# Score products one period behind their operands, norms and softmax in more pieces, W' blocks stored from two tiles

## The chip, the core and the metric

The kernel runs on one core of a Trainium2 chip. The core's engines each work through a queue of their own, in order: TensorE for matmuls (PE in the profile, its weight loads PEld), VectorE (DVE), ScalarE (ACT), GpSimd (POOL) and SyncE (SP), which here issues every DMA. The metric is the device time of one launch in microseconds, lower is better.

## What is computed

Two steps of a network, in float32, for B = 4 batches of N = 6080 tokens and C = 256 channels: an attention between channels, and a feed-forward layer of width 2048 on its result.

```python
qn = q / (np.linalg.norm(q, axis=1, keepdims=True) + 1e-06)
kn = k / (np.linalg.norm(k, axis=1, keepdims=True) + 1e-06)
s = kn.transpose(0, 2, 1) @ qn / tau
s = s - s.max(-1, keepdims=True)
a = np.exp(s)
a /= a.sum(-1, keepdims=True) + 1e-09
x = (v @ a).reshape(B * N, C)
h = x @ w_in
out = np.maximum(0.01 * h, h) @ w_out
```

The scores s of a batch are 256 x 256 and sum over all 6080 tokens, so a batch's attention matrix a is known only when all its q and k have been read.

## The kernel before

**Folding.** v @ a @ w_in is computed as v @ W', with W' = a @ w_in made once per batch. So the main loop multiplies v, laid out channel by token, with W' (256 x 2048), applies the leaky step, and multiplies with w_out.

**Precision.** Each float32 operand is split into a high part (a cast to float32r) and a low part (the rest), and a product takes three matmul passes: high by high, high by low, low by high. Splits cost ACT or DVE a cast and DVE a subtraction.

**Tiles and periods.** Tokens come in 24 tiles, six per batch: five of 2 x 512 and one of 2 x 480. For each tile the hidden width is walked in eight pairs p. One pass of the body of the inner loop is called a period here; a batch has 48 of them. A period computes four hidden blocks (C11, C22, C21, C12) by seven products of blocks (`block_product`, L517, three matmuls each) instead of eight: A11, S2, S3 and A22 add up in the bank ps_x, A12 goes to ps_y, S1 and S4 to ps_z. ACT copies ps_x away in between (`taken`, L544), DVE adds ps_y or ps_z (`add`, L538), and `leaky` does the activation and the split on ACT (L528, L529) and DVE (L531). The 24 matmuls with w_out (`ffn_out`, L563) run one period later; a period's PE queue has them in portions of 5, 5, 8 and 6 between the blocks (`out(n)`). At the end of a tile, finished outputs are copied to o_sb (L575) and stored.

**What is fitted in.** While a batch's 48 periods run, the next batch's scores are made: 48 chunks of 128 tokens. For each chunk ACT casts q and k (`cast`, L154) and squares them (L146), DVE subtracts (`low`, L158) and sums the squares (L149), and PE multiplies (`product`, L176) into the bank ps_s. Then come the norms by Newton steps (`norms`), the scaling of the scores and softmax (`scaled`, `exps`, `normed`), four transposes (`turn`, L279), and W' in four blocks j: two products per block (L383), two sums of sub-blocks, and for each of two pairs p = 2j and 2j + 1 the parts `begin` (blocks A11, A12 and A22, declared 1.0) and `rest` (S1 to S4, declared 1.2). Each pair's seven blocks, high and low, are stored to w_dram, and `w_load` brings them back as the tile w_split when the main loop needs them. Batch 0 uses its first W' blocks straight from w_split.

**What sets the order.** These steps wait in queues `todo` for ACT, DVE and PE, each with a declared length. `slot(queue, room)` takes steps off the head of a queue as long as the head's length fits into the room that is left; a head that doesn't fit holds back what is behind it. A step may put further steps, also at the head. In one period the slots lie like this (adds and leaky steps in their places):

```python
add(y); slot("dve", 1.3); out(5); slot("pe", 1); leaky(C11); slot("dve", 2.2)
S2; taken; slot("act", 1.8); S1; out(5); slot("pe", 1); S3; taken; add(z); slot("dve", 1.3)
out(8); slot("pe_late", 1); leaky(C22); A22; S4; add(z); leaky(C21); slot("dve", 0.8); leaky(C12)
```

`at(w, ...)` lists what is put into the queues at the start of period w. The opening, ahead of the first period, has batch 0's scores and the first block of W'; the conversion of w_in and w_out from 64 to 32 bits runs in it and in the first periods. Instructions outside these chains (loads, stores, the copies to o_sb) are placed by the framework's scheduler. An instruction waits until the buffer that it overwrites is free: w_new has two buffers, the high and the low half of one pair.

Of the kernel before, what the change touches and what calls it, by code (L numbers as in the profile page):

```python
# [31 lines left out]
def channel_attention_ffn(  # L32
# [17 lines left out]
    nc = tc.nc  # L50
# [49 lines left out]
    def f32(ap):  # L100
        return ap.bitcast(F32)


    class Scores:
# [10 lines left out]
        def begin(self, acc, s):  # L115
            self.acc, self.s = acc, s
# [83 lines left out]
                    )  # L200
            return mm

        def norms(self):
            n = 2 * CH
            x = small.tile([P, n], F32, name="nx")
            nc.vector.tensor_copy(out=x, in_=self.n_ps[:, 0:n])
# [4 lines left out]
            y = small.tile([P, n], F32, name="ny")  # L211
            nc.vector.tensor_scalar(
                out=y.bitcast(I32), in0=half, scalar1=-1.0, scalar2=RSQRT_MAGIC, op0=ALU.mult, op1=ALU.add
            )
            t = small.tile([P, n], F32, name="nt")
            for _ in range(3):
                nc.vector.tensor_tensor(out=t, in0=x, in1=y, op=ALU.mult)
                nc.vector.scalar_tensor_tensor(out=t, in0=t, scalar=-0.5, in1=y, op0=ALU.mult, op1=ALU.mult)
                nc.vector.scalar_tensor_tensor(out=y, in0=t, scalar=1.5, in1=y, op0=ALU.add, op1=ALU.mult)
            nc.vector.tensor_tensor(out=t, in0=x, in1=y, op=ALU.mult)  # L220
            nc.vector.tensor_scalar(out=t, in0=t, scalar1=1e-6, scalar2=None, op0=ALU.add)
            rn = small.tile([P, n], F32, name="rn")
            nc.vector.reciprocal(out=rn, in_=t)
            self.rk = small.tile([P, CH], F32, name="rk")
            nc.vector.tensor_scalar(
                out=self.rk, in0=rn[:, CH:n], scalar1=rtau[:, 0:1], scalar2=None, op0=ALU.mult
            )
            self.diag = small.tile([P, CH, P], F32, name="diag")
            for h in range(CH):
                last = nc.vector.tensor_scalar(  # L230
                    out=self.diag[:, h, :], in0=ident, scalar1=rn[:, h:h + 1], scalar2=None, op0=ALU.mult
                )
            return last

        def rows_mm(self):
# [4 lines left out]
                )  # L240
            return mm

        def scaled(self):
            self.rq = small.tile([P, C], F32, name="rq")
            nc.vector.tensor_copy(out=self.rq, in_=self.r_ps[:, 0:C])
            s = small.tile([P, CH, C], F32, name="s_sb")
            for h in range(CH):
                nc.vector.scalar_tensor_tensor(
                    out=s[:, h, :], in0=self.s[:, h * C:(h + 1) * C], scalar=self.rk[:, h:h + 1], in1=self.rq,
                    op0=ALU.mult, op1=ALU.mult,  # L250
                )
            self.nm = small.tile([P, CH], F32, name="nm")
            self.e = s
            return nc.vector.tensor_reduce(out=self.nm, in_=s, axis=AX.X, op=ALU.max, negate=True)
# [68 lines left out]
    class Conversions:  # L323
# [9 lines left out]
        def split(self):  # L333
            raw, split = self.loaded.pop(0)
            split(raw)
# [63 lines left out]
    def w_parts(b, j):  # L399

        HT = TW // 2
        a = [a_sb[b, j, h] for h in range(CH)]
        a21, a11, a22, a12 = a[0][:, 0:HT], a[0][:, HT:TW], a[1][:, 0:HT], a[1][:, HT:TW]
        s12, s34 = w_tmp("w_s"), w_tmp("w_s")
        s1, s2, s3, s4 = s12[:, 0:HT], s12[:, HT:TW], s34[:, 0:HT], s34[:, HT:TW]

        def sums(*of):
            for out, x, y, op in of:
                last = nc.vector.tensor_tensor(out=out, in0=x, in1=y, op=op)
            return last  # L410
# [5 lines left out]
        def split(k, w, *blocks):  # L416
            ks = slice(k * P, (k + 1) * P)
            for src, x0, n in blocks:
                src = src[:, ks] if n == 1 else src.rearrange(two, s=2)[:, :, ks]
                hi, lo = (x.rearrange(two, s=NS)[:, x0:x0 + n, :] for x in w)  # L420
                hi, lo = (x[:, 0, :] if n == 1 else x for x in (hi, lo))
                nc.vector.tensor_copy(out=hi, in_=src)  # L422
                last = nc.vector.tensor_tensor(out=lo, in0=src, in1=f32(hi), op=ALU.subtract)
            return last

        for k in range(2):
            p, w = 2 * j + k, []

            def begin(k=k, w=w, p=p):
                if b == 0:  # L430
                    w_split[0, p] = w_tile()
                    w += [w_split[0, p][:, x].rearrange("p s f -> p (s f)") for x in range(2)]
                else:
                    w += [work.tile([P, NS * P], F32R, name="w_new", bufs=2) for _ in range(2)]
                return split(k, w, (a11, A11, 1), (a[1], A22, 2))
# [141 lines left out]

    todo = {"act": deque(), "dve": deque(), "pe": deque(), "pe_late": deque()}  # L580
    steps = {}

    def at(w, fn, *args):
        steps.setdefault(w, []).append((fn, args))
# [10 lines left out]
    def put(queue, length, fn, then=(), first=False):  # L595


        def run():
            ins = fn()
            for entry in then:  # L600
                if entry[0] == "call":
                    entry[1](*entry[2:])
                else:
                    put(*entry)
            return ins

        (todo[queue].appendleft if first else todo[queue].append)((length, run))
# [102 lines left out]
    for b in range(1, B):  # L710
        w0 = (b - 1) * WPB
        sc = scores[b]
        done = FILL * G if b == 1 else 0
        begin_at, span = (NPAIR, 26) if b == 1 else (2, 32)
        when = {j: w0 + begin_at + (j - done) * span // (NCHUNK - done) for j in range(done, NCHUNK)}
        for i in range(done // G, len(sc.groups)):
            at(max(w0, when[i * G] - 3), lambda sc=sc, i=i: sc.load(i, qk_raw()))
        for j in range(done, NCHUNK):
            at(when[j], chunk_work, sc, j)
        e = w0 + begin_at + span + 1  # L720
        at(e, norm_work, sc)
        at(e + 1, row_work, sc)
        at(e + 2, turn_work, sc)
        at(e + 1, win_load, 0)
        at(e + 3, w_work, b, 0)


    sc, nxt = scores[0], scores[1]
# [30 lines left out]
            conv.split()  # L759
    sc.sums()  # L760
    sc.norms_mm()
    after["dve"] = sc.norms()
    with tc.issue_after(after["load"].ins):
        for i in range(min(2, FILL)):
            nxt.load(i, qk_raw())
    sc.rows_mm()
    after["scaled"] = sc.scaled()
    sc.exps()
    after["normed"] = sc.normed()
# [114 lines left out]
```

## Time and profile before

| | |
|---|---|
| three runs | 2280.37, 2281.03, 2281.41 us, median 2281.03 |
| the profiled execution | 2281.35 us |
| its span, first to last instruction | 2279.6 us |
| mean granted clock of TensorE | 0.987 |
| DMA | 324.74 MB, 142 GB/s over the span |
| idle time of PE in the first 200 us, longest group | 15.9 us in 4 waits for DVE's w_split |

The profile gives, for one execution, each engine's busy time, the chain of work that ended last, groups of instructions by line with their mean duration and the idle time of the engine just ahead of them, and who waited for whom. A wait is put down to the semaphore that came last. A row of the timeline has start, length, engine, line, operation, tiles (written, then read), shape, count, and in brackets the idle time ahead and what ended it.

### The profile page before, as it was taken

To read this page: it belongs to the slowest core of one execution; us is meant where nothing else is said; L and a number is where in the kernel's file an instruction comes from. 1 tells how busy PE (TensorE), PEld (TensorE's weight loads), DVE (VectorE), ACT (ScalarE), POOL (GpSimd) and SP (SyncE) were. 2 spreads that over 40 slices of the span, in tenths; PEclk is the share of its full clock that TensorE was granted. 3 is DMA by queue.
4 is the path that set the end of the run, shared out by engine and by line. 5 is a ranking of instruction groups with operands and counts; after the bars stand their busy time and mean duration, and the time that the engine had idled before them with its cause. 6 is when DMAs were issued, how large, how long until landed. Compare 5 with 4: busy or idle time off the path is not lost.

```text
span 2279.6 us, 27326 instructions
## 1 busy us (share of the span) xinstructions
PE 2204.1 (97%) x9940; PEld 1820.4 (80%) x9940; DVE 1494.0 (66%) x2651; ACT 1491.0 (65%) x2563; POOL 2.8 (0%) x10
## 2 busy tenths in 40 slices
PE   9689999999999999999999999999999999999999
PEld 7467888887878888888787888888788788888887
DVE  7986667666666666666666666676657555655554
ACT  6556767765557777776556777777655566666665
POOL 0000000000000000000000000000000000000000
PEclk9799999999999999999999999999999999999999
DMA  9435344342653434434364344343354432332331
GB/s 355 142 140 194 118 144 143 131 146 85 231 184 109 155 127 136 155 114 139 136 215 150 119 145 163 109 155 126 118 180 153 149 118 97 118 134 81 133 106 44
DMA packets 93975, 324.74 MB, mean 142 GB/s; under 512 B 10385, under 2 KB 16017, under 8 KB 93841
## 3 DMA queue, kind: packets, MB, share of 16 engines
q1 hardware_dynamic: 93840, 323.00, 40.8%
q8 instruction: 78, 1.28, 0.2%
q14 instruction: 57, 0.46, 0.1%
HBM read 264.50 MB, written 58.46 MB: 142 GB/s over the span
## 4 chain that ended last, share of the span: by engine, by line
PE 82%; DVE 10%; ACT 5%; DMA 1%; issue 1%; SPq 0%; DVEq 0%
PE ps_o L563 38%; PE ps_x L517 20%; PE ps_z L517 10%; PE ps_y L517 5%; PE ps_s L176 4%; DVE h L538 3%; DVE g_split L531 3%; ACT h L528 2%; ACT g_split L529 2%; PE ps_o L171 2%; PE ps_s L383 1%; DMA w_dram<-w_new 1%; ACT h L544 1%; DVE qk_split L158 1%; DMA f_raw<-in_w_out_dram 0%
## 5 line engine op out<-in xcount | busy, mean ns | idle before, releaser
L563 PE MATMUL ps_o<-g_split,w_out_split 128*128 128x512 f32 (+1 forms) x4608 | 1178.8, 392 | 0.0
L563 PEld LDWEIGHTS ps_o<-g_split,w_out_split 128*128 128x128 f32 x4608 | 870.7, 189 | 181.0
L531 DVE TENSOR_TENSOR g_split<-h,g_split 128x512 fp32r<-128x512 f32 (+1 forms) x768 | 525.6, 684 | 373.0 <-ACT g_split L529 371.2
L517 PE MATMUL ps_x<-v_split,w_split 128*128 128x512 f32 (+1 forms) x2304 | 660.8, 395 | 32.4 <-DVE w_split L422 15.9
L544 ACT COPY h<-ps_x 128x512 f32<-128x512 f32 (+1 forms) x576 | 334.7, 581 | 366.7 <-PE ps_x L517 365.8
L528 ACT ACTIVATE h<-h 128x512 f32<-128x512 f32 (+1 forms) x576 | 362.1, 629 | 321.8 <-DVE h L538 321.4
L517 PEld LDWEIGHTS ps_x<-v_split,w_split 128*128 128x128 f32 x2304 | 425.0, 190 | 124.0 <-ACT h L544 16.9
L529 ACT CAST g_split<-h 128x512 fp32r<-128x512 f32 (+1 forms) x768 | 473.5, 617 | 24.1
L538 DVE TENSOR_TENSOR h<-ps_z,h 128x512 f32<-128x512 f32 (+1 forms) x384 | 262.1, 683 | 342.1 <-ACT h L544 336.4
L517 PE MATMUL ps_z<-v_split,w_split 128*128 128x512 f32 (+1 forms) x1152 | 326.2, 392 | 15.6 <-DVE h L538 15.6
L517 PEld LDWEIGHTS ps_z<-v_split,w_split 128*128 128x128 f32 x1152 | 217.3, 189 | 65.0 <-DVE h L538 18.1
L517 PE MATMUL ps_y<-v_split,w_split 128*128 128x512 f32 (+1 forms) x576 | 164.4, 394 | 0.6 <-ACT w_a L393 0.6
L538 DVE TENSOR_TENSOR h<-ps_y,h 128x512 f32<-128x512 f32 (+1 forms) x192 | 131.5, 685 | 4.9 <-PE ps_y L517 3.0
L176 PEld LDWEIGHTS ps_s<-qk_split 128*128 128x128 f32 x804 | 113.9, 188 | 25.5 <-DVE qk_split L158 14.7
L176 PE MATMUL ps_s<-qk_split 128*128 128x256 f32 x804 | 123.2, 285 | 8.1 <-DVE qk_split L158 8.1
L517 PEld LDWEIGHTS ps_y<-v_split,w_split 128*128 128x128 f32 x576 | 110.4, 192 | 24.1 <-ACT w_a L393 1.1
L528 ACT ACTIVATE h<-ps_x 128x512 f32<-128x512 f32 (+1 forms) x192 | 113.2, 590 | 8.8 <-PE ps_x L517 8.6
L482 DVE TENSOR_TENSOR v_split<-v_raw,v_split 128x512 fp32r<-128x512 f32 (+1 forms) x144 | 98.7, 687 | 4.7
L149 DVE TENSOR_TENSOR sq_acc<-sq_acc,sq 128x512 f32<-128x512 f32 x141 | 96.4, 684 | 0.0
L158 DVE TENSOR_TENSOR qk_split<-qk_raw,qk_split 128x512 fp32r<-128x512 f32 x134 | 91.8, 685 | 0.0
L146 ACT ACTIVATE sq<-qk_raw 128x512 f32<-128x512 f32 x141 | 88.5, 632 | 1.4 <-DMA qk_raw<-in_k_dram 1.4
L154 ACT CAST qk_split<-qk_raw 128x512 fp32r<-128x512 f32 x134 | 82.9, 619 | 0.0
(101 smaller groups left out, 729.2 us busy)
## 6 DMA issues: line engine op xcount, KB each, us to landing
w_split<-w_dram SPq DMA_DIRECT2D x184, 896.0 KB, 4.6
qk_raw<-in_q_dram SPq DMA_DIRECT2D x92, 256.0 KB, 3.5
qk_raw<-in_k_dram SPq DMA_DIRECT2D x92, 256.0 KB, 3.9
w_dram<-w_new SPq DMA_DIRECT2D x48, 448.0 KB, 2.9
v_raw<-in_vT_dram SPq DMA_DIRECT2D x40, 512.0 KB, 5.7
out_dram<-o_sb SPq DMA_DIRECT2D x80, 256.0 KB, 3.4
win<-win_dram SPq DMA_DIRECT2D x24, 512.0 KB, 3.7
w_dram<-w_split SPq DMA_DIRECT2D x16, 448.0 KB, 3.5
```

The lines of the kernel that those rows point to most:

```text
L146: return nc.scalar.activation(out=out, in_=self.chunk(j), func=AF.Square)
L149: return nc.vector.tensor_tensor(out=self.acc[0], in0=self.acc[0], in1=sq, op=ALU.add)
L158: return nc.vector.tensor_tensor(out=sp[:, :, 1, :], in0=self.chunk(j), in1=f32(sp[:, :, 0, :]), op=ALU.subtract)
L176: mm = nc.tensor.matmul(out=s, lhsT=sp[:, 1, y, hs], rhs=sp[:, 0, z, :], start=False, stop=last and n == 2, skip_group_check=True,)
L482: last = nc.vector.tensor_tensor(out=sp[:, 1, 0:w], in0=src, in1=f32(sp[:, 0, 0:w]), op=ALU.subtract)
L517: mm = nc.tensor.matmul(out=ps[:, 0:n], lhsT=w[:, x, a, :], rhs=sp[:, y, 0:n], start=first and k == 0, stop=k == 2, skip_group_check=True,)
L528: nc.scalar.activation(out=out[:, 0:n], in_=h[:, 0:n], func=AF.Prelu, alpha=0.01)
L529: issued["act"] = nc.scalar.copy(out=sp[:, 0, 0:n], in_=out[:, 0:n])
L531: issued["dve"] = nc.vector.tensor_tensor(out=sp[:, 1, 0:n], in0=out[:, 0:n], in1=f32(sp[:, 0, 0:n]), op=ALU.subtract)
L538: issued["dve"] = nc.vector.tensor_tensor(out=h[:, 0:n], in0=ps[:, 0:n], in1=h[:, 0:n], op=ALU.add)
L544: issued["act"] = nc.scalar.copy(out=h[:, 0:n], in_=ps[:, 0:n])
L563: issued["pe"] = nc.tensor.matmul(out=o_ps[i][j][h][:, 0:n], lhsT=wo[:, x, f, h * P:(h + 1) * P], rhs=sp[:, y, 0:n], start=p == 0 and earl ...
```

## The change

Score products go to a queue of their own, `pe_next`, which is emptied into PE's queue at the start of the next period. The norms become three steps (the copy out of PSUM, two Newton steps, the rest) and the softmax's scaling two, with declared lengths of 1.8 and 2.0 for the long ones and 1.1 for the division. The scores of a batch are spread over one period less, while norms, rows, transposes and W' are put at e, e + 2, e + 4 and e + 5, against e, e + 1, e + 2 and e + 3 before, with e one period earlier. For batches 1 to 3 a pair's seven W' blocks go to two tiles of one buffer each, w_first (three blocks, high and low) and w_rest (four), each stored by one DMA as soon as it is full; batch 0 stores a pair by one DMA for two. No arithmetic is changed.

```diff
-        def norms(self):
-            n = 2 * CH
-            x = small.tile([P, n], F32, name="nx")
-            nc.vector.tensor_copy(out=x, in_=self.n_ps[:, 0:n])
+        def norms_taken(self):
+            self.nx = small.tile([P, 2 * CH], F32, name="nx")
+            return nc.vector.tensor_copy(out=self.nx, in_=self.n_ps[:, 0:2 * CH])
+
+        def newton(self, x, y, t, n):
+            for _ in range(n):
...
+        def norms_begun(self):
+            x, n = self.nx, 2 * CH
             half = small.tile([P, n], I32, name="nhalf")
...
-            for _ in range(3):
...
+            return self.newton(x, self.ny, self.nt, 2)
+
+        def norms(self):
+            x, y, t, n = self.nx, self.ny, self.nt, 2 * CH
+            self.newton(x, y, t, 1)
...
+        def rows_taken(self):
+            self.rq = small.tile([P, C], F32, name="rq")
+            return nc.vector.tensor_copy(out=self.rq, in_=self.r_ps[:, 0:C])
+
         def scaled(self):
-            self.rq = small.tile([P, C], F32, name="rq")
-            nc.vector.tensor_copy(out=self.rq, in_=self.r_ps[:, 0:C])
...
-            def begin(k=k, w=w, p=p):
+            def blocks(x0, n, name, k=k, w=w, p=p):
+
+                if b == 0:
+                    return [w_split[0, p][:, x, x0:x0 + n, :] for x in range(2)]
+                w.append(work.tile([P, 2, n, P], F32R, name=name, bufs=1))
+                return [w[-1][:, x] for x in range(2)]
+
+            def store(x0, n, w=w, p=p):
+                if b:
+                    nc.sync.dma_start(
+                        out=w_dram[b, p][:, :, x0 * P:(x0 + n) * P],
+                        in_=f32(w[-1].rearrange("p x s f -> p x (s f)")),
+                    )
+
+            def begin(k=k, p=p, blocks=blocks, store=store):
                 if b == 0:
                     w_split[0, p] = w_tile()
-                    w += [w_split[0, p][:, x].rearrange("p s f -> p (s f)") for x in range(2)]
-                else:
-                    w += [work.tile([P, NS * P], F32R, name="w_new", bufs=2) for _ in range(2)]
-                return split(k, w, (a11, A11, 1), (a[1], A22, 2))
-
-            def rest(k=k, w=w, p=p):
-                last = split(k, w, (s12, S1, 2), (s34, S3, 2))
-                for x in range(2):
-                    nc.sync.dma_start(out=w_dram[b, p][:, x], in_=f32(w[x]))
+                x0 = min(A11, A22)
+                last = split(k, blocks(x0, 3, "w_first"), x0, (a11, A11, 1), (a[1], A22, 2))
+                store(x0, 3)
+                return last
+
+            def rest(k=k, p=p, blocks=blocks, store=store):
+                last = split(k, blocks(S1, 4, "w_rest"), S1, (s12, S1, 2), (s34, S3, 2))
+                store(S1, 4)
+                if b == 0:
+                    w = w_split[0, p]
+                    nc.sync.dma_start(
+                        out=w_dram[0, p].rearrange("p x f -> p (x f)"), in_=f32(w.rearrange("p x s f -> p (x s f)"))
+                    )
                 return last
...
-            ("dve", 0.75, lambda: sc.low(j), [("pe", 1, lambda: sc.product(j))]),
+            ("dve", 0.75, lambda: sc.low(j), [("pe_next", 1, lambda: sc.product(j))]),
...
-        put("pe_late", 1, sc.norms_mm, [("dve", 0.5, sc.norms, (), True)])
+        put("pe_late", 1, sc.norms_mm, [
+            ("dve", 0.5, sc.norms_taken, [("dve", 1.8, sc.norms_begun, [("dve", 2.0, sc.norms)], True)], True),
+        ])
...
-            ("dve", 0.5, sc.scaled, [("act", 0.6, sc.exps, [("dve", 0.6, sc.normed, (), True)], True)], True),
+            ("dve", 0.5, sc.rows_taken, [
+                ("dve", 1.8, sc.scaled, [("act", 0.6, sc.exps, [("dve", 1.1, sc.normed, (), True)], True)], True),
+            ], True),
...
-        begin_at, span = (NPAIR, 26) if b == 1 else (2, 32)
+        begin_at, span = (NPAIR, 25) if b == 1 else (2, 31)
...
-        at(e + 1, row_work, sc)
-        at(e + 2, turn_work, sc)
+        at(e + 2, row_work, sc)
+        at(e + 4, turn_work, sc)
         at(e + 1, win_load, 0)
-        at(e + 3, w_work, b, 0)
+        at(e + 5, w_work, b, 0)
...
         for p in range(NPAIR):
+            todo["pe"].extend(todo["pe_next"])
+            todo["pe_next"].clear()
```

The next rows are DVE's queue at three places, before and in the change (L531 becomes L560, L538 becomes L567, L575 becomes L604). In these rows h is a hidden block, g_split its split after the leaky step.

First, from the leaky steps that close period 36 of batch 0's 48 on into the next, the softmax of batch 1. Before:

```order
L245 COPY rq<-ps_y 128x256
L248 SCALAR_TENSOR_TENSOR s_sb<-ps_s,rk,rq 128x256 x2
L254 TENSOR_REDUCE nm<-s_sb 128x2
L531 TENSOR_TENSOR g_split<-h,g_split 128x512
L538 TENSOR_TENSOR h<-ps_y,h 128x512
L267 TENSOR_SCALAR den<-den 128x2
L268 RECIPROCAL den<-den 128x2
L270 TENSOR_SCALAR s_sb<-s_sb,den 128x256 x2
```

In the change:

```order
L255 COPY rq<-ps_y 128x256
L560 TENSOR_TENSOR g_split<-h,g_split 128x512
L567 TENSOR_TENSOR h<-ps_y,h 128x512
L560 TENSOR_TENSOR g_split<-h,g_split 128x512
L260 SCALAR_TENSOR_TENSOR s_sb<-ps_s,rk,rq 128x256 x2
L266 TENSOR_REDUCE nm<-s_sb 128x2
L567 TENSOR_TENSOR h<-ps_z,h 128x512
L279 TENSOR_SCALAR den<-den 128x2
L280 RECIPROCAL den<-den 128x2
L282 TENSOR_SCALAR s_sb<-s_sb,den 128x256 x2
```

The scaling moved from ahead of a period's last leaky step to behind the next period's first one, and the division behind that period's first addition from ps_z.

Second, in period 40, the first of the batch's last tile (480 wide), from the leaky step of C11 on; w_a and w_s are blocks and sums of W'. Before:

```order
L531 TENSOR_TENSOR g_split<-h,g_split 128x480
L422 CAST w_new<-w_s 128x256 x2
L423 TENSOR_TENSOR w_new<-w_s,w_new 128x256 x2
L575 COPY o_sb<-ps_o 128x512
L422 CAST w_new<-w_a 128x128
L422 CAST w_new<-w_a 128x256
L423 TENSOR_TENSOR w_new<-w_a,w_new 128x128
L423 TENSOR_TENSOR w_new<-w_a,w_new 128x256
L538 TENSOR_TENSOR h<-ps_z,h 128x480
```

In the change:

```order
L560 TENSOR_TENSOR g_split<-h,g_split 128x480
L433 CAST w_first<-w_a 128x128
L433 CAST w_first<-w_a 128x256
L434 TENSOR_TENSOR w_first<-w_a,w_first 128x128
L434 TENSOR_TENSOR w_first<-w_a,w_first 128x256
L433 CAST w_rest<-w_s 128x256 x2
L434 TENSOR_TENSOR w_rest<-w_s,w_rest 128x256 x2
L567 TENSOR_TENSOR h<-ps_z,h 128x480
L604 COPY o_sb<-ps_o 128x512
```

A pair's two parts now follow each other behind the leaky step, and the addition from ps_z stands ahead of the copy to o_sb; the next pair's first part comes behind that copy.

Third, in the next batch's first period, where the last pair of W' (p = 7) is made behind the rest of pair 6. Before:

```order
L422 CAST w_new<-w_s 128x256 x2
L423 TENSOR_TENSOR w_new<-w_s,w_new 128x256 x2
L531 TENSOR_TENSOR g_split<-h,g_split 128x512
L422 CAST w_new<-w_a 128x128
L422 CAST w_new<-w_a 128x256
L575 COPY o_sb<-ps_o 128x480
L423 TENSOR_TENSOR w_new<-w_a,w_new 128x128
L423 TENSOR_TENSOR w_new<-w_a,w_new 128x256
L422 CAST w_new<-w_s 128x256 x2
L423 TENSOR_TENSOR w_new<-w_s,w_new 128x256 x2
L538 TENSOR_TENSOR h<-ps_z,h 128x512
```

In the change:

```order
L433 CAST w_rest<-w_s 128x256 x2
L434 TENSOR_TENSOR w_rest<-w_s,w_rest 128x256 x2
L560 TENSOR_TENSOR g_split<-h,g_split 128x512
L433 CAST w_first<-w_a 128x128
L433 CAST w_first<-w_a 128x256
L434 TENSOR_TENSOR w_first<-w_a,w_first 128x128
L434 TENSOR_TENSOR w_first<-w_a,w_first 128x256
L433 CAST w_rest<-w_s 128x256 x2
L434 TENSOR_TENSOR w_rest<-w_s,w_rest 128x256 x2
L567 TENSOR_TENSOR h<-ps_z,h 128x512
L604 COPY o_sb<-ps_o 128x480
```

The instructions stand as before, but in two tiles, and the copy to o_sb now comes behind the addition.

More of the change, by code (lines that the diff above doesn't have):

```diff
@@ L201, in norms_mm @@
             return mm
-        def norms(self):
-            n = 2 * CH
-            x = small.tile([P, n], F32, name="nx")
-            nc.vector.tensor_copy(out=x, in_=self.n_ps[:, 0:n])
+        def norms_taken(self):
[3 more added lines that the diff above has]
+            for _ in range(n):
+                nc.vector.tensor_tensor(out=t, in0=x, in1=y, op=ALU.mult)
+                nc.vector.scalar_tensor_tensor(out=t, in0=t, scalar=-0.5, in1=y, op0=ALU.mult, op1=ALU.mult)
+                last = nc.vector.scalar_tensor_tensor(out=y, in0=t, scalar=1.5, in1=y, op0=ALU.add, op1=ALU.mult)
+            return last
+        def norms_begun(self):
+            x, n = self.nx, 2 * CH
             half = small.tile([P, n], I32, name="nhalf")
@@ L210, in norms @@
             )
-            y = small.tile([P, n], F32, name="ny")
+            self.ny = small.tile([P, n], F32, name="ny")
             nc.vector.tensor_scalar(
-                out=y.bitcast(I32), in0=half, scalar1=-1.0, scalar2=RSQRT_MAGIC, op0=ALU.mult, op1=ALU.add
+                out=self.ny.bitcast(I32), in0=half, scalar1=-1.0, scalar2=RSQRT_MAGIC, op0=ALU.mult, op1=ALU.add
             )
-            t = small.tile([P, n], F32, name="nt")
-            for _ in range(3):
-                nc.vector.tensor_tensor(out=t, in0=x, in1=y, op=ALU.mult)
-                nc.vector.scalar_tensor_tensor(out=t, in0=t, scalar=-0.5, in1=y, op0=ALU.mult, op1=ALU.mult)
-                nc.vector.scalar_tensor_tensor(out=y, in0=t, scalar=1.5, in1=y, op0=ALU.add, op1=ALU.mult)
+            self.nt = small.tile([P, n], F32, name="nt")
+            return self.newton(x, self.ny, self.nt, 2)
+        def norms(self):
+            x, y, t, n = self.nx, self.ny, self.nt, 2 * CH
+            self.newton(x, y, t, 1)
             nc.vector.tensor_tensor(out=t, in0=x, in1=y, op=ALU.mult)
@@ L414, in w_parts, with split @@
         two = "p (s f) -> p s f"
-        def split(k, w, *blocks):
+        def split(k, to, at, *blocks):
             ks = slice(k * P, (k + 1) * P)
@@ L419, in split @@
                 src = src[:, ks] if n == 1 else src.rearrange(two, s=2)[:, :, ks]
-                hi, lo = (x.rearrange(two, s=NS)[:, x0:x0 + n, :] for x in w)
-                hi, lo = (x[:, 0, :] if n == 1 else x for x in (hi, lo))
+                hi, lo = (x[:, x0 - at, :] if n == 1 else x[:, x0 - at:x0 - at + n, :] for x in to)
                 nc.vector.tensor_copy(out=hi, in_=src)
@@ L427, in w_parts @@
             p, w = 2 * j + k, []
-            def begin(k=k, w=w, p=p):
+            def blocks(x0, n, name, k=k, w=w, p=p):
[10 more added lines that the diff above has]
+            def begin(k=k, p=p, blocks=blocks, store=store):
                 if b == 0:
                     w_split[0, p] = w_tile()
-                    w += [w_split[0, p][:, x].rearrange("p s f -> p (s f)") for x in range(2)]
-                else:
-                    w += [work.tile([P, NS * P], F32R, name="w_new", bufs=2) for _ in range(2)]
-                return split(k, w, (a11, A11, 1), (a[1], A22, 2))
-            def rest(k=k, w=w, p=p):
-                last = split(k, w, (s12, S1, 2), (s34, S3, 2))
-                for x in range(2):
-                    nc.sync.dma_start(out=w_dram[b, p][:, x], in_=f32(w[x]))
+                x0 = min(A11, A22)
+                last = split(k, blocks(x0, 3, "w_first"), x0, (a11, A11, 1), (a[1], A22, 2))
+                store(x0, 3)
+                return last
+            def rest(k=k, p=p, blocks=blocks, store=store):
[6 more added lines that the diff above has]
+                    )
                 return last
@@ L576, in ffn_out @@
                     nc.sync.dma_start(out=outT[h * P:(h + 1) * P, n0:n0 + n], in_=o[:, 0:n])
-    todo = {"act": deque(), "dve": deque(), "pe": deque(), "pe_late": deque()}
+    todo = {"act": deque(), "dve": deque(), "pe": deque(), "pe_late": deque(), "pe_next": deque()}
     steps = {}
@@ L761, in channel_attention_ffn @@
     sc.norms_mm()
+    sc.norms_taken()
+    sc.norms_begun()
     after["dve"] = sc.norms()
@@ L766, in channel_attention_ffn @@
     sc.rows_mm()
+    sc.rows_taken()
     after["scaled"] = sc.scaled()
```

## The prediction

> **What bounds the kernel now.** The page comes first: the span, the busy times and the chain that ended last.
>
> ```profile
> span 2279.6 us, 27326 instructions
> PE 2204.1 (97%) x9940; PEld 1820.4 (80%) x9940; DVE 1494.0 (66%) x2651; ACT 1491.0 (65%) x2563; POOL 2.8 (0%) x10
> PE 82%; DVE 10%; ACT 5%; DMA 1%; issue 1%; SPq 0%; DVEq 0%
> ```
>
> PE is busy for 97% and holds 82% of the chain; the other engines come into it only where PE stands. The change takes away no matmul, so all that it can win is PE's idle time and what follows from it. The waits of PE, cut at 200 us, say where that is (columns: total us, times, longest). This is all of PE's idle time behind 200 us:
>
> ```profile
> PE ps_z L517 <- DVE h L538: 15.6, 6, 3.8
> PE ps_s L176 <- DVE qk_split L158: 8.1, 18, 0.8
> PE ps_x L517 <- ACT h L544: 4.5, 3, 1.5
> PE ps_s L279 <- DVE s_sb L270: 4.1, 3, 1.4
> ```
>
> They sum to 32.3 us, and each group is one per batch or a few per tile. The waits ahead of 200 us belong to the opening, in which batch 0's scores, the weight conversion and the first W' run; there the order on PE, DVE and ACT is the same before and after, so I put that stretch at 0.
>
> To the idle time comes the clock. The table by windows gives, in its columns, the length, the busy time of PE, PEld, DVE, ACT and POOL with counts, the granted clock and the DMA share. The first three are the stretches behind the three longest waits; the fourth is the 3.41 us (half of what a drop lasts) ahead of the second of them, and the last holds most of the 2.47 us wait that ends at 580.25:
>
> ```profile
> 670.64:677.47 6.83, 5.87 (x14) 4.77 (x15) 4.07 (x7) 4.47 (x8) 0.00 (x0) 0.50 0.80 288
> 1227.01:1233.84 6.83, 6.16 (x15) 4.96 (x16) 3.77 (x7) 4.66 (x8) 0.00 (x0) 0.50 0.81 295
> 1783.39:1790.21 6.82, 6.04 (x15) 4.85 (x16) 3.88 (x7) 4.65 (x8) 0.00 (x0) 0.50 0.81 291
> 1223.60:1227.01 3.41, 1.19 (x6) 0.65 (x4) 2.68 (x10) 0.43 (x1) 0.00 (x0) 1.00 0.67 249
> 578.48:581.90 3.42, 1.66 (x7) 1.42 (x8) 2.68 (x8) 1.65 (x3) 0.00 (x0) 1.00 0.40 152
> ```
>
> Half clock for 5.87 + 6.16 + 6.04 = 18.07 us of matmuls costs half of that, 9.0 us. The stretch with 1.19 us of PE work lost the clock, the one with 1.66 us kept it. The ceiling is thus 32.3 + 9.0 = 41.3 us, 1.8% of the time.
>
> **Score products (8.1 us).** The low half of a chunk's split (L158) is computed just ahead of the product that reads it:
>
> ```profile
> 229.72 0.69 DVE L158 TENSOR_TENSOR qk_split<-qk_raw,qk_split 128x512 fp32r<-128x512 f32 x1
> 230.46 0.86 PE L176 MATMUL ps_s<-qk_split 128*128 128x256 f32 x5 [0.78 <-DVE qk_split L158]
> 510.57 0.84 PE L517 MATMUL ps_y<-v_split,w_split 128*128 128x512 f32 x3
> 511.25 1.31 PE L563 MATMUL ps_o<-g_split,w_out_split 128*128 128x512 f32 x5
> ```
>
> With the change a product enters PE's queue at the next period's start, and its first place there lies behind that period's ps_x and ps_y blocks and five output matmuls: the last two rows alone are 0.84 + 1.31 us. Even an L158 that closes a period is over by then. All 18 waits go: **-8.1**. The same matmuls remain, and a place without a product leaves 1.31 us of outputs between ps_y and the next ps_x block, against a copy (L544) of 0.59 us, as such places have now.
>
> **Norms (4.5 us) and softmax (4.1 us).** Now one piece of 17 small DVE instructions, declared 0.5, stands ahead of a leaky step, and everything behind it is late:
>
> ```profile
> 521.15 0.16 DVE L206 COPY nx<-ps_y 128x4 f32<-128x4 f32 x1
> 522.93 0.16 DVE L217 TENSOR_TENSOR nt<-nx,ny 128x4 f32<-128x4 f32 x1
> 524.27 0.48 DVE L230 TENSOR_SCALAR diag<-ident,rn 128x128 f32<-128x128 f32 x2
> 527.80 0.97 PE L517 MATMUL ps_x<-v_split,w_split 128*128 128x512 f32 x3 [1.50 <-ACT h L544]
> 534.17 0.88 DVE L248 SCALAR_TENSOR_TENSOR s_sb<-ps_s,rk,rq 128x256 f32<-128x256 f32 x2
> 535.80 0.51 ACT L259 ACTIVATE s_sb<-s_sb,nm 128x256 f32<-128x256 f32 x1 [0.66 <-DVE nm L254]
> 537.00 0.63 ACT L528 ACTIVATE h<-h 128x512 f32<-128x512 f32 x1
> 537.74 0.81 PE L279 MATMUL ps_s<-ident,s_sb 128*128 128x128 f32 x4 [1.37 <-DVE s_sb L270]
> 513.56 0.69 DVE L531 TENSOR_TENSOR g_split<-h,g_split 128x512 fp32r<-128x512 f32 x1 [1.35 <-ACT g_split L529]
> 515.82 0.59 ACT L544 COPY h<-ps_x 128x512 f32<-128x512 f32 x1 [1.81 <-PE ps_x L517]
> 516.44 0.69 DVE L538 TENSOR_TENSOR h<-ps_z,h 128x512 f32<-128x512 f32 x1 [2.19 <-ACT h L544]
> ```
>
> The pieces of the change fit only the slot of 2.2, which is where DVE idles: the last row shows 2.19 us of it in a period without score work. From 521.34 to 522.93 eight instructions take 1.6 us (norms begun); from 522.93 to 524.75 the rest takes 1.8 (norms); from 534.17 the scaling ends at about 535.8, 1.6. Each is under 2.19, so the wait of 1.50 goes three times: **-4.5**. The transposes (L279) wait now because the division ends in the same period, just ahead of them; in the change it ends in the period before: **-4.1**.
>
> What is late next is ACT. The exponentials (535.80 to about 536.9, 1.1 us) now stand between two copies L544. Laid over the rows at 513.56: the scaling ends at 514.2 + 1.6 = 515.8, the exponentials at 516.9, so the copy of 515.82 starts 1.1 us late. PE needs its end when the eight output matmuls are done, and the addition behind it half a microsecond later; I count 0.2 us of new wait, bounded by 0 and 1.1, three times: **+0.6**.
>
> **The first W' blocks of a batch (5.6 us).** The six waits on L538 come in two kinds. Three are in the first period of a batch's last tile, of 2.47, 1.58 and, by what the six sum to, 1.6 us:
>
> ```profile
> 577.17 0.69 DVE L575 COPY o_sb<-ps_o 128x512 f32<-128x512 f32 x1 [2.35 <-PE ps_o L563]
> 579.54 0.65 DVE L538 TENSOR_TENSOR h<-ps_z,h 128x480 f32<-128x480 f32 x1
> 580.25 0.92 PE L517 MATMUL ps_z<-v_split,w_split 128*128 128x480 f32 x3 [2.47 <-DVE h L538]
> 1137.27 0.92 PE L517 MATMUL ps_z<-v_split,w_split 128*128 128x480 f32 x3 [1.58 <-DVE h L538]
> ```
>
> DVE stands 2.35 us at a copy of a finished output, with the next pair's block and then the addition that PE wants queued behind it. In the order of the change the addition stands ahead of both. It then needs only what L538 needs elsewhere: at 516.44 it starts 2.6 us ahead of its ps_z matmuls. So the 5.6 us go. In return the copy and the block of about 1 us hold the leaky step behind them; the copy L544 of the next period has some 1 us to spare, so I add 0.2 each, bounded by 0 and 1: **-5.6 + 0.6 = -5.0**.
>
> **The last W' blocks, at a batch's end (10.0 us and the clock).** The other three waits are 3.84, 2.89 and 3.29 us:
>
> ```profile
> 668.15 0.43 DVE L422 CAST w_new<-w_a 128x128 fp32r<-128x128 f32 x2 [4.24 <-DMA w_dram<-w_new]
> 662.96 6.19 DMA w_dram<-w_new
> 669.25 0.63 DVE w_new L423 x2
> 671.60 1.65 PE L517 MATMUL ps_z<-v_split,w_split 128*128 128x512 f32 x3 [3.84 <-DVE h L538]
> 1227.68 1.65 PE L517 MATMUL ps_z<-v_split,w_split 128*128 128x512 f32 x3 [2.89 <-DVE h L538]
> 1784.17 1.65 PE L517 MATMUL ps_z<-v_split,w_split 128*128 128x512 f32 x3 [3.29 <-DVE h L538]
> ```
>
> The last pair overwrites both halves of w_new, and both stores lie behind the loads of a tile: the first landed at about 668.1 (the cast starts), the second at 669.15. In the order of the change the first three blocks find w_first free (stored periods ago) and are done under the wait. But the other four need w_rest, whose store goes out at the same point, behind the same loads. So the wait stays and gets shorter: 0.63 us of L423 leave the stretch behind the landing, and the landing moves. w_rest is 512 KB against 448 KB for a half; the two halves landed 1.1 us apart, so 64 KB more is 0.15 us, and it lands at about 668.25, 0.9 earlier. Each wait shrinks by 1.5 us, to 2.3, 1.4 and 1.8: **-4.5**. Bounds: landing with the first half gives -1.7 each. From the other side, packets of 2 KB in place of 3.5 KB are not shown for this store; the nearest are the output stores:
>
> ```profile
> w_dram<-w_new SPq DMA_DIRECT2D x48, 448.0 KB, 2.9
> out_dram<-o_sb SPq DMA_DIRECT2D x80, 256.0 KB, 3.4
> ```
>
> With less data these take 0.5 us longer, so the landing could be 669.6, and each wait would shrink by 0.2 alone. I take 1.5, nearer to the first row.
>
> Clock: waits of 1.4 and 1.8 us leave at least 1.6 us of PE work in any 3.41 us, like the stretch that kept it. A wait of 2.3 us inside one stretch leaves 1.1, like those that lost it. The drops stand 556.4 us apart, 163 times 3.413, so the stretches form a grid; the wait that began at 671.60 - 3.84 = 667.8 would begin 6.8 us earlier (four of the 18 score waits 1.8, then 1.5, 1.4 and 2.5, less 0.4), at 661.0; a grid line is at 660.4, so it would lie inside one stretch. So one drop stays, two go: **-6.1**, between 0 and -9.0.
>
> The page "TensorE: Matmul & The Clock Gate" of the Trainium skill, section "Why this matters for your kernels", advises against PE-idle gaps above roughly 3 us, since one idle window halves the clock. By that rule no shortened wait would cost the clock. The trace does not bear the limit out as it stands: a wait of 2.89 us lost it.
>
> **Elsewhere.** No DVE or ACT instruction is added. Batch 0's stores become 8 of 896 KB for 16 of 448 KB; nobody waits for them in the profile. DVE's 18.6 us at w_new in the middle of the production shrink, behind no wait of PE.
>
> **Sum** against the profiled execution's own 2281.35 us (0.3 us above the median 2281.03; span 2279.6): 8.1 + 4.5 + 4.1 - 0.6 + 5.0 + 4.5 + 6.1 = 31.7, so **2249.6 us**.
>
> **Rivals.**
> (a) All three drops go, with the other terms as above: 2.9 us more, 2246.7. For it: 2.3 us is below every wait that lost the clock. Against: the grid. This is the time that the rule on the page would give.
> (b) The store of w_rest lands at 669.6 and all three drops stay: the last two terms become 0.6 and 0, and 21.7 are won: 2259.7. For it: the loads ahead of it are unchanged. Against: less data than the two halves.
> (c) Part of the score waits comes back as waits for ACT or DVE once PE is ahead; with all of them back, 2257.7. Against: ACT and DVE are 65% and 66% busy, and they mostly wait for PE or each other.
> (d) Slower: the pieces of 1.8 and 2.0 at the head of DVE's queue hold back all that is queued behind them for four periods, the splits of the next tile's v among it. From the point where one of the last four splits stands behind the new tile's first period, PE waits for it: most of a period (10 of 556.4 / 48 = 11.6 us) and a clock drop (3 us) for each of three batches, 40 us: 2289.6. Against: in the order of the change these four still stand in the period ahead of that tile, where they stood.
> (e) The change doesn't do what it says, and waits only change places: within 0.2%, about 2280.
>
> **Chances.** Forecast 0.45, (a) 0.20, (b) 0.17, (c) 0.09, (d) 0.05, (e) 0.04. The range takes in the forecast, (a), (b), (c) and the bounds: with the waits at the batch ends gone altogether it would be 2281.35 - 41.3 + 1.2 = 2241; 2242 to 2262. A difference under 0.2% (4.6 us) can't be told from none: faster 0.91, same 0.04, slower 0.05.
>
> **What would show it.** In the profile after: no wait of ps_s on qk_split; no waits of 1.5 for L544 nor of 1.4 at the transposes; in the last tile's first period the addition ahead of the o_sb copy; at the batch ends three waits near 2.3, 1.4 and 1.8 us, released by a DVE that waited for w_rest's store, and one stretch at clock 0.50. The forecast is wrong if waits above 3 us remain there, if PE waits for v_split at a tile's start, or if new waits for L544 appear in most periods.

## The result, and the profile after

Four runs of the changed kernel gave a median of 2239.9 us (2238.8 to 2240.2), beside 2280.7 us for the kernel before: a ratio of 0.982, with a 95% interval of 0.9805 to 0.9834. The forecast was 2249.6 us, from 2242 to 2262, so the kernel is 9.7 us faster than predicted and lies just below the range. The profiled execution took 2239.86 us, 41.5 less than the one of before.

The page of the changed kernel: its span, its busy times and the engines' shares of the chain that ended last.

```profile
span 2238.1 us, 27253 instructions
PE 2189.6 (98%) x9940; PEld 1815.0 (81%) x9940; DVE 1492.8 (67%) x2651; ACT 1488.8 (67%) x2563; POOL 2.8 (0%) x10
PE 91%; DVE 5%; ACT 2%; DMA 1%; issue 0%; SPq 0%; DVEq 0%
```

PE's busy time fell too, by 14.5 us (2204.1 to 2189.6), although it executes the same 9940 matmuls. Of the four groups of waits behind 200 us this one is left (total us, times, longest):

```profile
PE ps_z L546 <- DVE h L567: 5.3, 3, 2.4
```

So 27.0 of the 32.3 us of idle time are gone, where the terms of the prediction net to 25.6. The three remaining waits stand at the batch ends (timeline of PE):

```profile
660.83 0.72 PE L546 MATMUL ps_z<-v_split,w_split 128*128 128x512 f32 x1 [2.15 <-DVE h L567]
1204.39 0.50 PE L546 MATMUL ps_z<-v_split,w_split 128*128 128x512 f32 x1 [2.43 <-DVE h L567]
1744.70 0.50 PE L546 MATMUL ps_z<-v_split,w_split 128*128 128x512 f32 x1 [0.70 <-DVE h L567]
```

Behind them is DVE's wait for w_rest's store. From the timeline of DVE, then the chain of the same stretch:

```profile
659.01 0.49 DVE L433 CAST w_rest<-w_s 128x256 fp32r<-128x256 f32 x2 [3.32 <-DMA w_dram<-w_rest]
659.42 0.75 DVE L434 TENSOR_TENSOR w_rest<-w_s,w_rest 128x256 fp32r<-128x256 f32 x2
660.09 0.68 DVE L567 TENSOR_TENSOR h<-ps_z,h 128x512 f32<-128x512 f32 x1
```

```profile
653.87 5.11 DMA w_dram<-w_rest
```

The first W' blocks of a batch do not hold the addition any more. This is DVE in the last tile's first period:

```profile
569.58 0.66 DVE L567 TENSOR_TENSOR h<-ps_z,h 128x480 f32<-128x480 f32 x1
570.82 0.69 DVE L604 COPY o_sb<-ps_o 128x512 f32<-128x512 f32 x1 [0.58 <-PE ps_o L592]
```

The clock, by the table of windows (length; busy time of PE, PEld, DVE, ACT and POOL with counts; granted clock; DMA share and GB/s):

```profile
657.53:660.94 3.41, 1.26 (x7) 0.72 (x6) 1.93 (x6) 0.52 (x2) 0.00 (x0) 1.00 0.42 155
660.94:664.35 3.41, 3.41 (x9) 2.77 (x10) 1.69 (x3) 2.32 (x5) 0.00 (x0) 0.50 0.87 276
664.35:667.76 3.41, 3.41 (x17) 2.81 (x16) 2.54 (x4) 2.50 (x5) 0.00 (x0) 1.00 0.94 356
1200.20:1203.61 3.41, 1.76 (x8) 1.13 (x7) 1.04 (x4) 0.56 (x1) 0.00 (x0) 1.00 0.60 215
1203.61:1207.02 3.41, 2.63 (x12) 2.24 (x13) 2.62 (x6) 2.62 (x6) 0.00 (x0) 1.00 0.62 216
```

The wait of 2.15 us lies inside one stretch, leaves it 1.26 us of work, and costs the clock, but for 3.41 us instead of 6.83. The longer one, of 2.43 us, is cut by the border at 1203.6 and costs nothing. Half clock for 3.41 us costs 1.7 us, against 9.0 before.

Idle time and clock behind 200 us explain 27.0 + 7.3 = 34.3 us. The waits ahead of 200 us sum to 38.7 us for 39.3, but nothing is won by that: in both traces PE starts its 701st matmul at 215.4 us. The end of the kernel costs 0.6 us more: from the start of the last matmul to the end of the span 4.7 us, for 4.1. So of 41.5 us, 7.8 are left. They must be in PE's busy time: behind 200 us it fell from 2043.5 to 2028.4 us, and 15.1 less the clock's 7.3 is 7.8. The rows of L176, before and after, show where the largest piece sits:

```profile
L176 PE MATMUL ps_s<-qk_split 128*128 128x256 f32 x804 | 123.2, 285 | 8.1 <-DVE qk_split L158 8.1
```

```profile
L176 PE MATMUL ps_s<-qk_split 128*128 128x256 f32 x804 | 117.9, 282 | 0.0
```

The same 804 matmuls take 5.3 us less once nothing makes them wait. One product in the timelines of PE tells how. Before (the row at 230.46, shown in the prediction, stands between these two), and after:

```profile
229.40 0.28 PE L176 MATMUL ps_s<-qk_split 128*128 128x256 f32 x1
...
231.16 0.86 PE L517 MATMUL ps_x<-v_split,w_split 128*128 128x512 f32 x3
```

```profile
229.20 0.86 PE L176 MATMUL ps_s<-qk_split 128*128 128x256 f32 x6
229.91 0.85 PE L546 MATMUL ps_x<-v_split,w_split 128*128 128x512 f32 x3
```

From the product's start to the start of what follows it are 1.76 us before and 0.71 after: the wait cost 1.05 us, and its row says 0.78. In a flow of matmuls each starts about 0.16 us ahead of the end shown for the one before it (six of 0.28 us stand in 0.86). At a wait that overlap is lost, which is 0.16 us. And the first matmul behind it lasts 0.39 us in the trace for 0.28, which is 0.11 more: the five behind the wait take 0.86 us, as long as six without one. Both are booked as busy time. The short score waits show the same: 0.19 us in the row, 0.46 from start to start. So each wait costs its row and 0.27 us, and the 27 waits that went were worth 7.3 us more than the prediction counted; 0.5 us of the 7.8 stay open. That was the theory to test.

### The profile page after: what moved, and what is told of

Same layout as the page of the kernel before. It is cut to its first block, busy times and chain, and to the rows that moved or that the text cites. A ratio compares the mean times of both kernels' runs of the same rounds, so it can differ in the third digit from the quotient of the medians.

```text
span 2238.1 us, 27253 instructions
## 1 busy us (share of the span) xinstructions
PE 2189.6 (98%) x9940; PEld 1815.0 (81%) x9940; DVE 1492.8 (67%) x2651; ACT 1488.8 (67%) x2563; POOL 2.8 (0%) x10
## 4 chain that ended last, share of the span: by engine, by line
PE 91%; DVE 5%; ACT 2%; DMA 1%; issue 0%; SPq 0%; DVEq 0%
PE ps_o L592 44%; PE ps_x L546 22%; PE ps_z L546 11%; PE ps_y L546 5%; PE ps_s L176 4%; PE ps_o L171 2%; PE ps_s L395 1%; DVE h L567 1%; DVE g_split L560 1%; ACT h L557 1%; ACT g_split L558 1%; DMA w_dram<-w_rest 1%; DMA f_raw<-in_w_out_dram 0%; DVE w_split L434 0%; DVE v_split L511 0%; DVE f_x L328 0%
## 5 line engine op out<-in xcount | busy, mean ns | idle before, releaser
L560 DVE TENSOR_TENSOR g_split<-h,g_split 128x512 fp32r<-128x512 f32 (+1 forms) x768 | 525.4, 684 | 396.1 <-ACT g_split L558 394.6
L567 DVE TENSOR_TENSOR h<-ps_z,h 128x512 f32<-128x512 f32 (+1 forms) x384 | 262.0, 682 | 293.1 <-ACT h L573 286.5
L567 DVE TENSOR_TENSOR h<-ps_y,h 128x512 f32<-128x512 f32 (+1 forms) x192 | 131.3, 684 | 1.9
L176 PEld LDWEIGHTS ps_s<-qk_split 128*128 128x128 f32 x804 | 114.0, 188 | 12.1 <-issue 1.0
L176 PE MATMUL ps_s<-qk_split 128*128 128x256 f32 x804 | 117.9, 282 | 0.0
```

Source lines behind the costliest of these rows:

```text
L176: mm = nc.tensor.matmul(out=s, lhsT=sp[:, 1, y, hs], rhs=sp[:, 0, z, :], start=False, stop=last and n == 2, skip_group_check=True,)
L560: issued["dve"] = nc.vector.tensor_tensor(out=sp[:, 1, 0:n], in0=out[:, 0:n], in1=f32(sp[:, 0, 0:n]), op=ALU.subtract)
L567: issued["dve"] = nc.vector.tensor_tensor(out=h[:, 0:n], in0=ps[:, 0:n], in1=h[:, 0:n], op=ALU.add)
```

## Experiments

In what follows, the **idle theory** says that a wait costs what its row shows, and the **restart theory** that it costs 0.27 us more.

**The score products alone** (b_scores), in the kernel before:

```diff
-            ("dve", 0.75, lambda: sc.low(j), [("pe", 1, lambda: sc.product(j))]),
+            ("dve", 0.75, lambda: sc.low(j), [("pe_next", 1, lambda: sc.product(j))]),
...
         for p in range(NPAIR):
+            todo["pe"].extend(todo["pe_next"])
+            todo["pe_next"].clear()
```

> The kernel before, with nothing but the score products moved to the next period's start. Idle theory (a wait of PE costs what its idle row shows): the 18 waits of 8.1 us go, L176's busy time stays at 123.2 us, 2280.7 - 8.1 = 2272.6 us. Restart theory (each wait also costs 0.16 us of overlap with the matmul ahead of it and 0.11 us in a longer first matmul behind it, both booked as busy time): 18 x 0.27 = 4.9 us more, L176's busy time falls to about 118, 2267.7 us. Both: the waits of ps_z for DVE and the three clock drops stay.

Measured: 2268.6 us, beside 2281.6 for the kernel before; ratio 0.9942 (0.9929 to 0.9954). That is 13.0 us, what the restart theory gives; the idle theory's 8.1 us would be a ratio of 0.9964, outside the interval. The page's row of L176 and the waits behind 200 us:

```profile
L176 PE MATMUL ps_s<-qk_split 128*128 128x256 f32 x804 | 118.0, 282 | 0.0
```

```profile
PE ps_z L517 <- DVE h L538: 17.5, 6, 4.2
PE ps_x L517 <- ACT h L544: 4.5, 3, 1.5
PE ps_s L279 <- DVE s_sb L270: 4.1, 3, 1.4
PE ps_s L383 <- ACT w_a L393: 0.2, 1, 0.2
```

The product's idle time and 5.2 us of its busy time went together, 13.3 us; the other waits stayed, those of ps_z 1.9 us longer. The whole span does not close as well: the idle rows behind 200 us fell by 6.0 us, 17 waits fewer are 4.6, and the clock cost 0.4 more, which makes 10.2 us, and the span is 11.7 shorter. The rest of 1.5 us is open. By the idle theory the rest would be 6.1 us.

**The portions alone** (b_portions): the kernel after with the old issue of the products (as in a_scores_old below) and the old w_new and its two stores.

> The kernel after, with the score products and the W' tiles and stores of before: the norms and the softmax in portions, one period less for the scores, W' one period later. In this program's order the addition from ps_z stands ahead of the copy to o_sb in the first period of each batch's last tile, as in the kernel after. Idle theory: the waits of 4.5, 4.1 and 5.6 us go, 2280.7 - 14.2 = 2266.5 us. Restart theory: 9 waits x 0.27 = 2.4 us more, 2264.1 us. Both: 18 score waits of 8.1 us and the batch-end waits of about 10 us with their three clock drops stay. If instead the 5.6 us came from the W' tiles, 2272.1 (idle) or 2270.5 (restart).

Measured: 2260.4 us, ratio 0.9902 (0.9887 to 0.9918), 21 us for the 14 to 17 expected. The execution that was profiled took 12467 us, for 2257.7 to 2261.2 of the other three: in its trace PE is busy for 12455.7 us with the same 9940 matmuls, and why is open. Its waits can't be compared, so the same program ran again:

> The same program as b_portions, for its trace. It was 21 us faster than before, against 14.2 (idle) and 16.6 (restart). The theory for the rest: W' stands a period later here, so that the last pair's stores meet another point of the tile loads and the batch-end waits are shorter than 10.0 us, and one clock drop or more is gone (3 us each). The trace should show no wait of ps_x for L573's copy, none at the transposes, none in the last tile's first period, 18 score waits of 8.1 us, and batch-end waits of 5 to 9 us in total.

Measured: 2257.0 us beside 2280.7, ratio 0.9901 (0.9885 to 0.9918). Its waits behind 200 us:

```profile
PE ps_z L529 <- DVE h L550: 11.6, 3, 4.2
PE ps_s L176 <- DVE qk_split L158: 2.8, 7, 0.8
PE ps_x L529 <- ACT h L556: 1.2, 3, 0.4
PE ps_s L395 <- ACT w_a L405: 1.0, 3, 0.3
```

The expectation missed on three points. Of the 18 score waits only 7 are left: presumably the other spacing of the scores (one period less) puts fewer subtractions just ahead of their product; it was not changed alone. The batch-end waits are longer (11.6 us), not shorter. And two clock drops of 3.41 us, 3.4 us, took the place of 9.0. Idle rows 15.7 us, clock 5.6, and 14 waits x 0.27 = 3.8 sum to 25.1, against 24.9 us between the two spans (2279.6 and 2254.7).

**W' in two tiles alone** (b_tiles), the change's `split`, `blocks`, `store`, `begin` and `rest` in the kernel before:

> The kernel before, with nothing but W' in two tiles and its stores. The addition stands ahead of the copy here too. Idle theory: 5.6 us go, the batch-end waits shrink from 10.0 to 5.3 us, and the clock keeps 7.5 of 9.0 us if two of three drops go and one halves: 2280.7 - 17.8 = 2262.9 us. Restart theory: 3 x 0.27 more, 2262.1 us. If the clock drops depend on where a wait falls among stretches of 3.41 us, their number here may differ from that of the kernel after, by up to 3 us each.

Measured: 2269.9 us, ratio 0.9947 (0.9935 to 0.996): 11.7 us for 17.8. Of its waits, the score products' 8.1 us and the groups of 4.5 and 4.1 us stand as before, and the rest is:

```profile
PE ps_z L534 <- DVE h L555: 8.5, 6, 2.3
```

The batch ends shrank as expected, to 5.3 us, but 3.1 us of the 5.6 in the last tile's first period stayed (1.78, 0.41 and 0.92). The addition does stand ahead of the copy; what holds it is now a store, by the timeline of DVE:

```profile
578.31 0.43 DVE L421 CAST w_first<-w_a 128x128 fp32r<-128x128 f32 x2 [3.16 <-DMA w_dram<-w_first]
578.65 0.62 DVE L422 TENSOR_TENSOR w_first<-w_a,w_first 128x128 fp32r<-128x128 f32 x2
579.19 0.65 DVE L555 TENSOR_TENSOR h<-ps_z,h 128x480 f32<-128x480 f32 x1
```

In this program the next pair's first block is ahead of the addition. In the kernel after, W' comes a period later, and the block stands behind it. Thus the 5.6 us belong to both parts: the portions alone leave no wait of ps_z there, but short ones of 0.39 and 0.35 us; only together is there none.

**The last pair's rest later** (a_rest_late), in the kernel after:

```diff
-            yield 1.2, rest
+            yield 1.2 if p < NPAIR - 1 else 1.3, rest
```

> The kernel after, with the last pair's rest declared 1.3 in place of 1.2, which puts it behind the addition from ps_z. DVE then waits for w_rest's store with nothing behind it that PE needs within 3 us. The three batch-end waits (2.15, 2.43, 0.70) go, and the one clock drop. Idle theory: 2239.9 - 5.3 - 1.5 = 2233.1 us. Restart theory: 3 x 0.27 more, 2232.3 us. If the store holds the leaky steps behind it long enough, a wait for g_split of a few tenths appears in the next period instead.

Measured: 2233.3 us, ratio 0.979 (0.9777 to 0.9804). All of PE's waits behind 200 us:

```profile
PE ps_x L546 <- ACT h L573: 0.3, 1, 0.3
```

The addition now goes first, and DVE waits behind it (timeline of DVE):

```profile
656.87 0.69 DVE L567 TENSOR_TENSOR h<-ps_z,h 128x512 f32<-128x512 f32 x1 [1.20 <-ACT h L573]
658.66 0.49 DVE L433 CAST w_rest<-w_s 128x256 fp32r<-128x256 f32 x2 [1.10 <-DMA w_dram<-w_rest]
```

The store landed 0.35 us earlier (658.66 for 659.01), which is little; it is now waited for where PE doesn't need DVE. From 155 us to the last 2 us the clock stayed at 1.00. The two theories stand 0.8 us apart here (2233.1 and 2232.3), too little to tell them apart. A second comparison, beside the kernel after on one chip:

> The same program as a_rest_late, beside the kernel after on one chip: 2233.3 us, no clock drop behind the opening, PE's idle time behind 200 us 0.3 us.

> The kernel after again: 2239.8 us, three batch-end waits of 5 to 6 us in total. By the windows seen so far a wait costs the clock only if a stretch of 3.41 us has less than 1.66 us of PE work, which depends on where the stretches fall in the execution: 0 to 2 drops of 3.41 us.

Measured: 2233.3 us, ratio 0.9797 (0.9784 to 0.9811), and 2241.3 us, ratio 0.9829 (0.9816 to 0.9842). The version with the later rest beats both kernels: the kernel after by 8.0 us here, and its other medians by 6.4 and 6.6.

**Products at once** (a_scores_at_once), a dose of waits in the kernel after:

```diff
-            ("dve", 0.75, lambda: sc.low(j), [("pe_next", 1, lambda: sc.product(j))]),
+            ("dve", 0.75, lambda: sc.low(j), [("call", product, sc, j)]),
...
+    def product(sc, j):
+        with in_order("pe"):
+            issued["pe"] = sc.product(j)
```

> The kernel after, with each score product put on PE's queue at the very point where its subtraction L158 stands on DVE's, so that PE reaches most of them before the operand is there: many waits of PE in place of 18. With N waits more than in the kernel after and I us more idle time of PE in the trace, the idle theory gives 2239.9 + I and the restart theory 2239.9 + I + 0.27 N, as long as no clock drop comes in. Estimate: one wait for most of the 124 products behind the opening, of about 1 us each, N = 100 and I = 100: 2340 by the idle theory, 2367 by the restart theory. The spacing of two matmuls across a wait should be the wait + 0.16 us + the usual spacing, and the first matmul behind it 0.11 us longer.

Measured: 2548.3 us, ratio 1.1166 (1.1138 to 1.1193). The estimates of number and length were too low, and the clock came in after all. Span and the row of L176 of the page, then its waits:

```profile
span 2548.0 us, 27260 instructions
...
L176 PE MATMUL ps_s<-qk_split 128*128 128x256 f32 x804 | 158.5, 312 | 219.7 <-DVE qk_split L158 208.4
```

```profile
PE ps_s L176 <- DVE qk_split L158: 208.4, 134, 3.3
PE ps_s L176 <- ACT qk_split L154: 11.4, 18, 0.9
PE ps_z L546 <- DVE h L567: 5.7, 3, 2.6
```

The span grew by 309.9 us. Idle time behind 200 us grew by 225.5 - 5.3 = 220.2, and 32 stretches of 3.41 us at half clock for one make 52.9: together 273.1, and 36.8 us are missing by the idle theory. For 152 waits more that is 0.24 us each; the restart theory's 0.27 gives 41.0. L176's own busy time, 158.5 against 117.9 us, grew by 0.27 us per wait. So the extra cost follows the number of waits, not their length.

Most of the gap between 0.24 and 0.27 is the clock, which was taken as costing half of a slow stretch. Five matmuls in such a stretch, from the start of the first to the start of the next block (timeline of PE):

```profile
224.38 2.33 PE L592 MATMUL ps_o<-g_split,w_out_split 128*128 128x512 f32 x5
226.52 1.00 PE L546 MATMUL ps_x<-v_split,w_split 128*128 128x512 f32 x3
```

They start 0.43 us apart, for 0.23 at full clock (three in 0.68 us from 510.57 to 511.25, in the prediction's rows), so a slow stretch loses 46% of its time. The 31 stretches then cost about 49 us, 41 are missing, and that is 0.27 for each wait. By the same 46%, the clock's 9.0 and 1.7 us are 8.4 and 1.6, which leaves 0.5 us more of the 41.5 open.

**The products as before, in the kernel after** (a_scores_old), with the kernel after beside it:

```diff
-            ("dve", 0.75, lambda: sc.low(j), [("pe_next", 1, lambda: sc.product(j))]),
+            ("dve", 0.75, lambda: sc.low(j), [("pe", 1, lambda: sc.product(j))]),
```

> The kernel after, with the score products issued as before (behind their subtraction, in the same period). If each part is worth in the kernel after what it was worth alone, 18 waits and 13 us come back: 2253. If the other schedule of the scores (31 and 25 periods for 32 and 26) has taken most of these waits by itself, as in the second trace of the portions alone, 7 waits of 2.8 us come back: 2239.9 + 2.8 = 2242.7 by the idle theory, + 7 x 0.27 = 2244.6 by the restart theory. A batch-end wait at another place among the stretches of 3.41 us can add or take 1.7 us of clock each.

> The kernel after, unchanged, beside the one with the old issue of the score products, so that the two are compared on one chip: 2239.9 us, PE's idle time behind 200 us 5.3 us in three waits, one clock drop of 3.41 us.

Measured: 2246.0 us, ratio 0.9852 (0.9836 to 0.9869), and 2239.7 us, ratio 0.9825 (0.9811 to 0.984). The waits of the first:

```profile
PE ps_z L546 <- DVE h L567: 5.8, 3, 2.7
PE ps_s L176 <- DVE qk_split L158: 2.5, 7, 0.8
```

Seven waits came back, not 18: in the kernel after, the new issue of the products is worth 6.3 us, of which 2.5 + 7 x 0.27 = 4.4 are the waits; the trace also has two clock drops (3.4 us), where that of a_again has none. The 11 others go with the portions as well as with the new issue. This is one reason why the three parts alone sum to about 47 us (13, 21 to 24, and 12) and together give 41.

## Why the prediction was wrong

It named the right waits, and nearly every one behaved as it said. What failed is a step ahead of all terms, in its first part: "all that it can win is PE's idle time and what follows from it", and with it "the ceiling is thus 32.3 + 9.0 = 41.3". The kernel won 41.5 us with 5.3 us of waits and 1.7 us of clock still there. The step took a wait for its idle row; each costs 0.27 us more. The range's lower end was worked out from that ceiling, so it was too high as well. Of the 9.8 us by which the forecast fell short, 7.3 are these restarts, 1.2 the clock, 1.2 new waits that were added and did not come, and 0.2 the batch ends; the end of the kernel takes 0.6 back, and 0.5 stay open. Term by term, in us of the profiled executions:

| term | predicted | measured |
|---|---|---|
| score products | -8.1 | -8.1, and 18 restarts: -4.9 |
| norms | -4.5 + 0 | -4.5, and 3 restarts: -0.8 |
| transposes | -4.1 + 0.6 | -4.1, no new wait, and 3 restarts: -0.8 |
| first W' blocks | -5.6 + 0.6 | -5.6, no new wait, and 3 restarts: -0.8 |
| batch ends | -4.5 | 10.0 to 5.3: -4.7 |
| clock | -6.1 | 9.0 to 1.7: -7.3 |
| opening | 0 | 0 |
| end of the kernel | 0 | +0.6 |
| sum | -31.7 | -41.0; the executions differ by 41.5 |

- **Score products.** The mechanism was right: no product waits. The term was mis-sized by 4.9 us, shown by the products alone and by the dose. It also stood on all 18 waits; without the new issue of the products, the rest of the change still removes 11 of them.
- **Norms and softmax.** Both waits went three times. The new wait of 0.2 us for ACT did not come. The timelines of ACT and PE of the changed kernel:

```profile
535.41 0.49 ACT L271 ACTIVATE s_sb<-s_sb,nm 128x256 f32<-128x256 f32 x1
535.81 0.19 ACT L271 ACTIVATION_READ_ACCUMULATOR s_sb<-s_sb,nm 128x1 f32 x1
535.90 0.56 ACT L573 COPY h<-ps_x 128x512 f32<-128x512 f32 x1
```

```profile
534.73 2.01 PE L592 MATMUL ps_o<-g_split,w_out_split 128*128 128x512 f32 x8
536.57 0.91 PE L546 MATMUL ps_x<-v_split,w_split 128*128 128x512 f32 x3
```

  The copy ends at 536.46, and PE's next block starts at 536.57, when the eight output matmuls let it: the delay used up the slack and no more.
- **First W' blocks.** All three waits went, but the reason given, the addition ahead of the copy, was half of it: W' in two tiles alone has that order and keeps 3.1 us.
- **Batch ends.** 2.3, 1.4 and 1.8 us were predicted, 2.15, 2.43 and 0.70 came: the sum holds (5.5 and 5.3), the single landings do not. The bounds cover them but for the third.
- **Clock.** One drop of three, as predicted, and inside one stretch, as predicted. It lasted 3.41 us, not 6.83: before, part of the wait reached into the slow stretch, now none does. And that it is one is chance: the wait began 9.1 us earlier than before (658.68 for 667.76), not 6.8, since the seven waits ahead of it cost 1.9 us of restarts, the four score waits among them have rows of 1.9 us and not 1.8, and the 0.4 us of new waits did not come. And the stretches do not start with the program. Of three executions of the kernel after that were profiled, one had one drop, one none and one two.
- **Rivals.** All three drops gone (a) is how one of the three executions ended. The late store (b) would have shortened each batch-end wait by 0.2 us; they shrank by 1.7, 0.5 and 2.6, so it is nearly true of the second alone. The return of score waits (c) and the late splits of v (d) did not occur: no row of PE waits for v_split or for qk_split behind 200 us. The time itself rules out (e). Where the score products did turn into a new wait is ACT, whose cast now waits for a buffer that a later product reads, and PE sees nothing of it:

```profile
ACT qk_split L154 <- PE ps_s L176: 24.6, 17, 2.0
```

## What to carry to other kernels

Count the waits of a busy PE as well as their time: from the start of the matmul ahead to the start of the one behind, less the usual spacing, is what a wait costs, and many short ones cost more than their idle rows. A wait for a DMA need not become shorter if it can be put behind the instruction that another engine needs; here one declared length did it. Parts of a change that are measured alone do not add up where they remove the same waits.

## What the runs showed of the hardware

**The restart.** 0.16 us of lost overlap and 0.11 us of longer first matmul, at waits from 0.19 to 2.5 us (behind longer ones the half clock lengthens the first matmul too; behind the waits at the transposes, of 128 columns, it is 0.05 us longer). Waits ahead of 512-column matmuls show the same overlap lost (0.15 to 0.17 us). The ends of matmuls in the profile are modelled; what was measured is starts, and why a first matmul is longer is not shown. The Trainium skill, page "TensorE: Matmul & The Clock Gate", section "Single matmul latency", gives a single bf16 matmul a constant of 166 ns at full clock on top of the columns' time. The traces agree with it in size for the first of the two pieces, 0.16 us; that this is the same constant no run shows.

**The clock's rule.** In the eleven traces that were read, PE's busy time was summed in each stretch of 3.413 us behind 200 us, on the grid on which the clock changes. Of some 6600 stretches at full clock, all that kept it had at least 1.57 us of work, and of the 48 that lost it, 46 had at most 1.56 (the others 1.77 and 1.78, both in the dose of waits). A slow stretch with at least 3.15 us of work ended the drop (48 times); one with at most 2.79 us prolonged it (5 times). The nearest case, from the windows of the products at once:

```profile
220.01:223.42 3.41, 1.56 (x9) 1.43 (x10) 1.29 (x2) 0.47 (x1) 0.00 (x0) 1.00 0.02 5
223.42:226.83 3.41, 3.41 (x9) 2.65 (x9) 0.00 (x0) 2.15 (x4) 0.00 (x0) 0.50 0.00 0
```

So a wait of 2.4 us may or may not cost the clock, depending on whether the grid cuts it, and in these traces only a wait under about 1.6 us (3.41 - 1.78) was safe by its length alone, if no other lay in the same stretch. The same page of the Trainium skill, section "What's actually happening", says that the window is free-running and does not reset when a kernel starts; the three profiled executions of one program with one, no and two drops agree.
